# Attention and MLP on one core: a f32 first k half, a split first q half, and another order for the first batch

## The chip, the core and the metric

The kernel runs on one core of a Trainium2 chip. The metric is device time in microseconds (us); lower is better. The core has five engines that run side by side, each with its own list of instructions taken in order: TensorE (PE in the profile; its weight loads are PEld), VectorE (DVE), ScalarE (ACT), GpSimd (POOL) and SyncE (SP). An engine waits for another one, or for a transfer (DMA), by a semaphore. Transfers are issued here from POOL, SP and ACT.

## The reference

Eight batches of eight heads go through local attention (512 positions, window 32 to each side) with 32 global positions per head; both the local and the global rows attend to the global keys too. The result, 4352 tokens of 512 values, goes through an MLP with the activation h·sigmoid(1.702 h):

```python
s_g = scale * q_g @ [k_g, k_l].T ;  out_g = softmax(s_g) @ [v_g, v_l]
s_l = scale * [q_l @ k_g.T , where(|i-j| <= 32, q_l @ k_l.T, -1e9)]
out_l = softmax(s_l) @ [v_g, v_l]
x = concat([out_g, out_l], seq).transpose(0, 2, 1, 3).reshape(4352, 512)
h = x @ w_in ;  out = (h * sigmoid(1.702 h)) @ w_out        # 512 -> 2048 -> 512
```

The inputs and the output are float32; the kernel multiplies in bfloat16.

## The kernel before, in words

The work is cut into 16 "quads": batch b, four heads u = 0 or 1. In the code `a` is the quad with u = 0, `c` the one with u = 1. Each quad goes through these steps, each a method of `Quad`:

- `Tk`, `Tq` (L263, L266): VectorE turns k and q in blocks, from the loaded `rk`, `rq` into `kT` and `qt`. `ext` (L275): four small copies put the global queries at both ends of `qt`.
- `S(0)`, `S(1)` (L293, L302): scores of two windows each on TensorE, into the four-bank PSUM tile `s4`, of which there is one (`psS`, one buffer). Only the first `S(1)` of all uses four single banks instead (`split=True`).
- `X` (L314, L312): exponentials on ScalarE into `e`; `M` (L321): VectorE multiplies them by `mask`.
- `K`, `XK` (L326, L332): scores of the global keys and their exponentials `ek`.
- `U(0)`, `U(1)`, `U(2)` (L341, L349): sums of the exponentials, and the two halves of e·v, each into one bank `ov`; `Gm` (L367): the global rows, into `og`.
- `R` (L373 to L377): reciprocals of the sums; `XL` (L382): the normalised x into `xL`; `G` (L387 to L390): the same for the global rows into `xG`.

The single banks (`kb`, `ov`, `og`, `hp`, `op`) come from one pool, `psP`, of four buffers taken in turn; a user of a bank waits for what read it four allocations before.

When a batch has its `xL`, the MLP follows. `h_step(i, fc)` for fc = 0 to 15 makes one 128-wide slice of h (L414, four matmuls), its tanh on ScalarE (`th`, L421) and the product on VectorE (`gT`, L422). In batch 0 the first four slices are different: `h_mm` puts them into one `s4` tile, tanh runs on two slices at once (L524) and `act4` (L458) makes two slices of `gT` in one instruction. `o_mm` (`osteps`) multiplies `gT` by w_out (L439): a step (tci, f4) is four matmuls, of fc = 4·f4 to 4·f4+3, into the bank `op` of row block tci; after the fourth step ScalarE copies the bank to `ob` (L446) and SP stores it. From batch 1 on, `phase_o` lays the attention of the next batch between the output matmuls of this one.

The order on each engine is the order of the calls in the source (`manual_schedule`). Nearly all loads are issued on POOL and cast to bf16 on the way (L84, L88, L97, L223, L225); each of them waits until the one eight places before it has landed. At the start the q half of batch 0, u = 0, comes as f32 (`q32`) on the ACT queue and ScalarE casts it (L465); `load_g32` brings the global rows of batches 0 and 1 as f32, and `cast_g32` (L121) casts them on VectorE. `make_mb` (L170) copies mask rows `mk` to four partition groups, `make_mask` (L177) spreads them into `mask`. `keep` issues matmuls without use (L152): 17 at the start, four before the first `S(1)`. The lines around the first batch that the change rewrites:

```python
    a.U(0)
    a.U(1)
    c.S(1)
    c.X(1)
    a.U(2)
    c.K()
    c.XK()
```

Of the kernel before, what the change touches and what calls it, by code (L numbers as in the profile page):

```python
# [12 lines left out]
F32 = mybir.dt.float32  # L13
BF16 = mybir.dt.bfloat16
FP8 = mybir.dt.float8e4
AF = mybir.ActivationFunctionType
# [4 lines left out]
def kernel(  # L21
# [12 lines left out]
    nc = tc.nc  # L34

    B, H, Sl, D = q_l.shape
# [20 lines left out]
    ld = ctx.enter_context(tc.tile_pool(name="ld", bufs=3))  # L57
# [7 lines left out]
    kf = k_l.rearrange("b (u j) (c r t) d -> b j r u c (t d)", j=4, c=4, t=4)  # L65
# [5 lines left out]
    loaded = {}  # L71

    def load(b, us=(0, 1), kq=True):
        if b not in loaded:
            loaded[b] = (ld.tile([128, 2, 4, 4 * D], BF16, name="rk"),
                         ld.tile([128, 2, 16 * D], BF16, name="rq"))
        if kq:
            for j in (0, 2, 1, 3):
                for u in us:
                    load_k(b, u, j)  # L80
            load_q(b, us)

    def load_k(b, u, j):
        nc.gpsimd.dma_start(out=loaded[b][0][32 * j : 32 * j + 32, u], in_=kf[b, j][:, u])  # L84

    def load_q(b, us):
        s = slice(us[0], us[-1] + 1)
        nc.gpsimd.dma_start(out=loaded[b][1][:, s], in_=qf[b][:, s])  # L88
# [14 lines left out]
    def load_g(lo, hi):  # L103
        nc.gpsimd.dma_start(out=rkg[:, lo:hi, :], in_=kgf[:, lo:hi, :])
        nc.gpsimd.dma_start(out=rqg[:, lo:hi, :], in_=qgf[:, lo:hi, :])
        nc.gpsimd.dma_start(out=rvg[:, lo:hi, :], in_=vgf[:, lo:hi, :])

    g32 = {}

    def load_g32(b, names, hold=False, eng=None):  # L110
        for name, s in (("q", qgf), ("k", kgf), ("v", vgf)):
            if name in names:
                t = g32[b, name] = consts.tile([128, 2, D], F32, name="g32%s%d" % (name, b))
                if hold:
                    nc.vector.memset(t[:, :, 0:1], 0.0)
                (eng or nc.sync).dma_start(out=t, in_=s[:, 2 * b : 2 * b + 2, :])

    def cast_g32(b, names):
        for name, t in (("q", rqg), ("k", rkg), ("v", rvg)):
            if name in names:  # L120
                nc.vector.tensor_copy(t[:, 2 * b : 2 * b + 2, :], g32[b, name])  # L121

    load_g32(0, "qk")

    q32 = ld.tile([128, 16 * D], F32, name="q32", bufs=1)
    nc.scalar.dma_start(out=q32, in_=qf[0][:, 0])
    load_g32(0, "v", eng=nc.scalar)
    load(0, kq=False)
    for j in range(4):
        load_k(0, 0, j)  # L130


    mk = consts.tile([32, 208], BF16)
    nc.vector.memset(mk, 1.0)
    for sg, base in ((1, 2 * W + 3), (-1, -3)):
        nc.gpsimd.affine_select(
            out=mk, in_=mk, pattern=[[-sg, 208]], compare_op=ALU.is_ge,
            fill=0.0, base=base, channel_multiplier=4 * sg,
        )
    load(0, (1,))  # L140

    w_in_sb = wts.tile([128, 2, NKC, d_ff // 2], BF16)
    w_out_sb = wts.tile([128, FC, d_model], BF16)
# [20 lines left out]
    mb = consts.tile([128, 16, 12], BF16)  # L164
# [2 lines left out]

    def make_mb():
        for k in range(4):
            nc.scalar.activation(mb[32 * k : 32 * k + 32],  # L170
                                 mk[:, 3 - k : 195 - k].rearrange("p (r t) -> p t r", t=16), AF.Copy)

    def make_mask():
        at = 0
        for c, (r0, nr) in enumerate(WIN):
            lo = r0 - 8 * c + 2
            nc.scalar.activation(  # L177
                mask[:, c // 2, at : at + 16 * nr].rearrange("p (t r) -> p t r", t=16),
                mb[:, :, lo : lo + nr], AF.Copy)
            at = (at + 16 * nr) % LW  # L180
# [7 lines left out]
    for i in range(2):  # L188
        v = consts.tile([128, 2, 4, 4, D + 2], BF16, name="v%d" % i)
# [14 lines left out]
    def transpose_g(lo, hi):  # L204
        for dst, s in ((kgT, rkg), (qgT, rqg)):
            nc.vector.transpose(dst[:, lo:hi, :32], s[:, lo:hi].bitcast(F32))

    def expand_g(b, which):
        qs = slice(2 * b, 2 * b + 2)
        kgBD, vgBD = GB[b % 3]  # L210
        out_, in_ = (kgBD, kgT[:, qs].bitcast(BF16)) if which == 0 else (vgBD[:, :, :, :D], rvg[:, qs])
        nc.vector.tensor_mul(
            out_,
            in_.rearrange("p n (o w) -> p n o w", o=1).to_broadcast([128, 2, 4, D]),
            bdm.rearrange("p (o j) w -> p o j w", o=1).to_broadcast([128, 2, 4, D]),
        )

    def load_rest():
        load_v(0)
        for part in range(2):  # L220
            cs = slice(part * (d_ff // 2), (part + 1) * (d_ff // 2))
            for u in range(2):
                nc.gpsimd.dma_start(out=w_in_sb[:, part, 2 * u : 2 * u + 2, :], in_=w_in_r[u][:, :, cs])  # L223
        for g4 in range(4):
            nc.gpsimd.dma_start(  # L225
                out=w_out_sb[:, 4 * g4 : 4 * g4 + 4, :].rearrange("p (g e) m -> p g (e m)", e=2),
                in_=w_out_r[:, 2 * g4 : 2 * g4 + 2, :])
            if g4 == 1:
                load(1, (0,))
        load(1, (1,))  # L230
        load_v(1, (0,))
        load_v(1, (1,))
        load(2)
# [7 lines left out]
    class Quad:  # L241
# [20 lines left out]
            cs = slice(128 * cs[0], 128 * cs[-1] + 128)  # L262
            nc.vector.transpose(self.kT[:, cs], rk[:, cs])  # L263

        def Tq(self):
            nc.vector.transpose(self.qt[:, 4:20, :].rearrange("p t r -> p (t r)"),  # L266
                                loaded[self.b][1][:, self.u].bitcast(F32))

        def T(self):
            self.Tk()  # L270
# [136 lines left out]
    def width(i):  # L407
        return TB if i < B else B * Sg
# [3 lines left out]
    def h_mm(i, fc, hp, kcs):  # L412
        for kc in kcs:
            nc.tensor.matmul(hp[:, : width(i)], lhsT=w_in_c[:, fc // 8, kc, fc % 8 // 2, :, fc % 2],  # L414
                             rhs=(xL[i] if i < B else xG)[:, kc, :],
                             start=(kc == 0), stop=(kc == NKC - 1))
# [8 lines left out]
    def h_step(i, fc):  # L425
        if fc == 0:
            gTs[i] = moe.tile([128, FC, TB], BF16, name="gT")
        hp = pbank("hp")
        h_mm(i, fc, hp, range(NKC))
        h_act(i, fc, hp)  # L430
# [25 lines left out]
    def act4(i, hf):  # L456
        f = slice(2 * hf, 2 * hf + 2)
        nc.vector.scalar_tensor_tensor(gTs[i][:, f, :], in0=th4s[i][:, f], scalar=1.0, in1=pts[i][:, f],  # L458
                                       op0=ALU.add, op1=ALU.mult)
# [2 lines left out]

    a, c = Quad(0), Quad(1)
    rk, rq = loaded[0]
    nc.scalar.activation(rq[:, 0], q32, AF.Copy)  # L465
    make_mb()
    make_mask()
    cast_g32(0, "qk")
    transpose_g(0, 2)
    a.ext()  # L470
    a.Tq()
    a.Tk((0, 1))
    a.Tk((2, 3))
    load_g32(1, "qkv", hold=True)
    load_rest()
    a.S(0)
    a.X(0)
# [1 line left out]
    a.S(1, split=True, warm=4)  # L479
    a.X(1)  # L480
    c.ext()
    cast_g32(0, "v")
    c.Tk()
    expand_g(0, 1)
    a.K()
    a.XK()
    a.M(0)
    c.Tq()
    c.S(0)
    c.X(0)  # L490
    a.M(1)
    a.U(0)
    a.U(1)
    c.S(1)
    c.X(1)
    a.U(2)
    c.K()
    c.XK()
    a.Gm()
    a.R()  # L500
    c.M(0)
    a.XL(0)
    a.XL(1)
    c.M(1)
    a.G()
    gTs[0] = moe.tile([128, FC, TB], BF16, name="gT")
    pt = pts[0] = psS.tile([128, 4, 512], F32, name="s4")
    for fc in (0, 1):
        h_mm(0, fc, pt[:, fc, :], (0, 1))
    for unit in range(3):  # L510
        c.U(unit)
    for fc in (2, 3):
        h_mm(0, fc, pt[:, fc, :], (0, 1))
    c.R()
    c.XL(0)
    c.XL(1)
    c.Gm()
    for kc in (2, 3):
        for fc in range(4):
            h_mm(0, fc, pt[:, fc, :], (kc,))  # L520
    th4 = th4s[0] = ld.tile([128, 4, TB], F32, name="th4", bufs=1)
    for hf in range(2):
        f = slice(2 * hf, 2 * hf + 2)
        nc.scalar.activation(th4[:, f], pt[:, f], AF.Tanh, scale=0.851)  # L524
    act4(0, 0)
    c.G()

    for fc in range(4, FC):
        h_step(0, fc)
        if fc == 8:  # L530
            cast_g32(1, "qkv")
        if fc == 11:
            transpose_g(2, 4)
    load_g(4, 8)
    load_v(2)
    load(3)

    def osteps(i, *sts):
        for tci, f4 in sts:
            o_mm(i, 4 * tci + f4)  # L540

    nq = {1: (Quad(2), Quad(3)), 2: (Quad(4), Quad(5))}
    a, c = nq[1]
    a.T()
    a.ext()
    act4(0, 1)
    expand_g(1, 0)
    c.ext()
    expand_g(1, 1)
    osteps(0, (0, 1), (1, 1), (2, 1), (0, 0))  # L550
    a.S(0)
    a.X(0)
    a.M(0)
    osteps(0, (1, 0), (2, 0))
    a.S(1)
    a.K()
    a.X(1)
    a.XK()
    a.M(1)
    osteps(0, (0, 2), (1, 2), (2, 2), (0, 3))  # L560
    c.T()
    c.S(0)
    c.X(0)
    c.M(0)
    osteps(0, (1, 3), (2, 3))
    c.S(1)
    c.K()
    c.X(1)
    c.XK()
    c.M(1)  # L570
    for unit in range(3):
        a.U(unit)
    a.Gm()
    a.R()
    a.XL(0)
    a.XL(1)
    a.G()
    c.UG()
    c.RXG()
    osteps(0, (3, 0), (3, 1), (3, 2), (3, 3))  # L580
    a, c = nq[2]
# [116 lines left out]
```

## Time and profile before

| What | us |
|---|---|
| median of 7 runs (lowest, highest) | 324.58 (322.83, 325.47) |
| the profiled execution, its own time | 322.73 |
| its span, first to last instruction | 321.0 |
| TensorE busy | 302.3 (94%) |
| VectorE busy | 214.4 (67%) |
| ScalarE busy | 167.2 (52%) |
| first attention score on TensorE starts | 7.63 |
| first `hp` slice (fc = 4 of batch 0) starts | 26.10 |
| first output matmul starts | 37.73 |
| first `hp` slice of batch 1 starts | 63.24 |

The span is what the profile covers; about 1.7 us of the execution's own time lie around it. A line of the profile names the engine, the line of the kernel, the operation, what it writes and reads, its shape, and in brackets how long the engine stood idle before it and what ended that. Times of instructions are from the start of the span. A matmul of 512 columns is shown as 379 ns long, but they overlap: sixteen of them run in 3.47 us (46.23 to 49.70), 0.217 us each.

### The profile page before, as it was taken

To read this page: it belongs to the slowest core of one execution; us is meant where nothing else is said; L and a number is where in the kernel's file an instruction comes from. 1 tells how busy PE (TensorE), PEld (TensorE's weight loads), DVE (VectorE), ACT (ScalarE), POOL (GpSimd) and SP (SyncE) were. 2 spreads that over 40 slices of the span, in tenths; PEclk is the share of its full clock that TensorE was granted. 3 is DMA by queue.
4 is the path that set the end of the run, shared out by engine and by line. 5 is a ranking of instruction groups with operands and counts; after the bars stand their busy time and mean duration, and the time that the engine had idled before them with its cause. 6 is when DMAs were issued, how large, how long until landed. Compare 5 with 4: busy or idle time off the path is not lost.

```text
span 321.0 us, 7295 instructions
## 1 busy us (share of the span) xinstructions
PE 302.3 (94%) x2956; PEld 147.7 (46%) x2997; DVE 214.4 (67%) x465; ACT 167.2 (52%) x252; POOL 79.0 (25%) x129
## 2 busy tenths in 40 slices
PE   8498988899999999999999999999999999999994
PEld 3253434444554454544554455445454454445551
DVE  7865954979766877678865876687857855484320
ACT  5725546077345655476446744565537733563421
POOL 8822596477019000720037000300000000000000
PEclk9979999999999999999999999999999999999999
DMA  8999999999929402990149311900211011101122
GB/s 156 165 201 207 205 119 147 176 147 128 124 65 156 76 10 60 104 156 4 42 69 166 59 35 45 120 2 6 61 36 34 2 35 50 51 0 31 36 65 65
DMA packets 59840, 27.40 MB, mean 85 GB/s; under 512 B 43168, under 2 KB 51360, under 8 KB 59808
## 3 DMA queue, kind: packets, MB, share of 16 engines
q0 software_dynamic: 51504, 17.11, 48.9%
q1 hardware_dynamic: 7888, 9.25, 10.7%
q10 hardware_dynamic: 416, 0.59, 0.6%
q8 instruction: 23, 0.38, 0.5%
q14 instruction: 9, 0.07, 0.1%
HBM read 35.13 MB, written 8.91 MB: 137 GB/s over the span
## 4 chain that ended last, share of the span: by engine, by line
PE 80%; DMA 7%; POOL 4%; DVE 3%; ACT 2%; issue 1%; POOLq 0%; DVEq 0%
PE op L439 35%; PE hp L414 32%; DMA w_out_sb<-in_moe_w_out_dram 5%; PE s L293 5%; PE ov L349 3%; PE ov L341 3%; POOL rk L84 2%; PE kb L326 2%; DMA rk<-in_k_l_dram 2%; ACT e L314 1%; POOL v L97 1%; POOL w_in_sb L223 1%; ACT ob L446 1%; DVE xL L382 1%; DVE sT L373 1%
## 5 line engine op out<-in xcount | busy, mean ns | idle before, releaser
L439 PE MATMUL op<-w_out_sb,gT 128*128 128x512 bf16 x516 | 122.2, 379 | 3.4 <-DVE gT L458 1.1
L422 DVE SCALAR_TENSOR_TENSOR gT<-th,hp 128x512 bf16<-128x512 f32 (+1 forms) x140 | 91.2, 656 | 47.1 <-ACT th L421 46.4
L414 PE MATMUL hp<-xL,w_in_sb 128*128 128x512 bf16 x487 | 108.2, 379 | 1.6 <-DVE xg L389 1.1
L421 ACT ACTIVATE th<-hp 128x512 f32<-128x512 f32 (+1 forms) x140 | 79.9, 573 | 43.2 <-PE hp L414 39.1
L414 PEld LDWEIGHTS <-w_in_sb 128*128 128x128 bf16 x576 | 56.0, 98 | 65.9 <-DVE xg L389 1.6
L439 PEld LDWEIGHTS <-gT 128*128 128x128 bf16 x544 | 51.9, 98 | 62.9 <-issue 4.0
L314 ACT ACTIVATE e<-s 128x1712 bf16<-128x1712 f32 x31 | 49.5, 1596 | 31.6 <-PE s L293 25.1
L446 ACT ACTIVATE ob<-op 128x512 f32<-128x512 f32 x34 | 20.2, 597 | 65.4 <-PE op L439 56.7
L97 POOL DMA_DIRECT2D v<-in_v_l_dram x36 | 27.0, 759 | 98.6 <-PE og L367 94.6
L84 POOL DMA_DIRECT2D rk<-in_k_l_dram x64 | 34.8, 550 | 19.1 <-DMA v<-in_v_l_dram 6.1
L321 DVE TENSOR_TENSOR e<-e,mask 128x1408 bf16<-128x1408 bf16 x32 | 28.0, 874 | 15.5 <-ACT e L314 15.3
L373 DVE STREAM_TRANSPOSE sT<-ov 128x512 f32<-128x512 f32 x16 | 11.4, 714 | 20.8 <-PE ov L349 20.8
L382 DVE TENSOR_TENSOR xL<-ov,rs 128x512 bf16<-128x512 f32 x32 | 20.7, 686 | 3.9 <-PE ov L349 2.3
L293 PE MATMUL s<-q,kT 32*128 32x200 bf16 (+1 forms) x512 | 21.4, 286 | 0.7 <-DVE q L266 0.7
L349 PE MATMUL ov<-e,v 128*32 128x192 bf16 (+1 forms) x512 | 15.7, 243 | 2.7 <-DMA v<-in_v_l_dram 2.7
L293 PEld LDWEIGHTS <-kT 32*128 32x128 bf16 x512 | 10.8, 96 | 10.7 <-issue 6.9
L349 PEld LDWEIGHTS <-v 128*32 128x32 bf16 x512 | 11.8, 98 | 6.6 <-issue 3.3
L341 PE MATMUL ov<-ek,vgBD 128*32 128x512 bf16 x128 | 12.7, 386 | 1.1 <-DVE xL L382 1.1
L377 DVE STREAM_TRANSPOSE rs<-rT 128x512 f32<-128x512 f32 x16 | 11.4, 712 | 0.6
L263 DVE STREAM_TRANSPOSE kT<-rk 128x512 f32<-128x512 f32 (+1 forms) x17 | 11.3, 668 | 0.0
L266 DVE STREAM_TRANSPOSE q<-rq 128x512 f32<-128x512 f32 x16 | 10.8, 673 | 0.0
L326 PE MATMUL kb<-q,kgBD 128*128 128x512 bf16 x29 | 9.4, 396 | 1.0 <-ACT e L312 0.7
(61 smaller groups left out, 148.7 us busy)
## 6 DMA issues: line engine op xcount, KB each, us to landing
out_dram<-ob SPq DMA_DIRECT2D x136, 64.0 KB, 1.8
rk<-in_k_l_dram POOLq DMA_DIRECT2D x64, 64.0 KB, 4.0
v<-in_v_l_dram POOLq DMA_DIRECT2D x28, 128.0 KB, 4.7
rq<-in_q_l_dram POOLq DMA_DIRECT2D x6, 512.0 KB, 7.2
w_in_sb<-in_moe_w_in_dram POOLq DMA_DIRECT2D x4, 512.0 KB, 11.2
w_out_sb<-in_moe_w_out_dram POOLq DMA_DIRECT2D x4, 512.0 KB, 12.8
rq<-in_q_l_dram POOLq DMA_DIRECT2D x3, 256.0 KB, 7.8
q<-in_q_l_dram ACTq DMA_DIRECT2D x1, 512.0 KB, 3.6
```

What stands on the lines that cost most here:

```text
L84: nc.gpsimd.dma_start(out=loaded[b][0][32 * j : 32 * j + 32, u], in_=kf[b, j][:, u])
L97: nc.gpsimd.dma_start(out=vtiles[b % 2][p, s, :, :, :D], in_=vf[b, t][:, hs])
L293: nc.tensor.matmul(ps[j][:, off : off + n * nr], lhsT=self.k[p, 128 * c : 128 * c + 128, e], rhs=self.q[p, t0 : t0 + n, r0 : r0 + nr, e], ...
L314: nc.scalar.activation(e[:, :, :RW], self.ps[:, :, :RW], AF.Exp, scale=scale)
L321: nc.vector.tensor_mul(e, e, mask[:, rnd : rnd + 1, :].to_broadcast([128, 4, LW]))
L349: nc.tensor.matmul(ov[32 * j : 32 * j + 32, :].rearrange("p (t r) -> p t r", t=16)[:, :, r0 : r0 + nr], lhsT=lv, rhs=self.E[c // 2][:, j, ...
L382: nc.vector.tensor_mul(self.x[:, 2 * self.u + h, :], self.st[1 + h], self.st["rs"])
L414: nc.tensor.matmul(hp[:, : width(i)], lhsT=w_in_c[:, fc // 8, kc, fc % 8 // 2, :, fc % 2], rhs=(xL[i] if i < B else xG)[:, kc, :], start=( ...
L421: nc.scalar.activation(th[:, :n], hp[:, :n], AF.Tanh, scale=0.851)
L422: nc.vector.scalar_tensor_tensor(gTs[i][:, fc, :n], in0=th[:, :n], scalar=1.0, in1=hp[:, :n], op0=ALU.add, op1=ALU.mult)
L439: nc.tensor.matmul(op, lhsT=gTs[i][:, fc, tci * 128 : tci * 128 + 128], rhs=w_out_sb[:, fc, :], start=(first and fc == 4 * f4), stop=(fc = ...
L446: nc.scalar.activation(ob, op, AF.Copy, scale=0.5)
```

## The change

It rewrites the prologue and the order of the calls of the first batch and a half; the loop from batch 1 on (`phase_o` and after) is untouched.

- **Loads.** The k half of batch 0, u = 0, is no longer cast on the way by four POOL loads but loaded as f32 (`k32`) by four loads on SP, the first that SP issues. Half of it is cast by ScalarE, half by VectorE. The global q and k of batch 0 move from SP to ACT, behind `q32`; the global v moves from ACT to SP. The POOL queue begins with the four k loads of u = 1. The global loads of batch 1 are called later, and `cast_g32` of batch 1 goes to ScalarE.
- **First q half.** Cast and turned in two pieces of 512 columns.
- **Mask rows.** The four copies of `make_mb` go from ScalarE to VectorE.
- **Order of the first batch.** `c.S(1)` goes ahead of `a.U(1)`, `c.K` ahead of it; `a.R` earlier; `c.M(1)` ahead of `a.XL`; the first `h_mm` all after `c.U`; `a.G` and `c.G` ahead of the first `act4`; the second tanh pair and `act4(0, 1)` from after the `h_step` loop to its place behind fc = 12.
- **First output phase.** The steps (tci, f4) are taken so that row blocks 0, 1 and 2 end one after the other. `c.T` goes ahead of `a.M(1)`, `c.M(1)` behind `a.R`.

```diff
     def cast_g32(b, names):
...
-                nc.vector.tensor_copy(t[:, 2 * b : 2 * b + 2, :], g32[b, name])
-
-    load_g32(0, "qk")
-
+                if b:
+                    nc.scalar.activation(t[:, 2 * b : 2 * b + 2, :], g32[b, name], AF.Copy)
+                else:
+                    nc.vector.tensor_copy(t[:, 2 * b : 2 * b + 2, :], g32[b, name])
+
+    load(0, kq=False)
     q32 = ld.tile([128, 16 * D], F32, name="q32", bufs=1)
+    k32 = ld.tile([128, 4, 4 * D], F32, name="k32", bufs=1)
     nc.scalar.dma_start(out=q32, in_=qf[0][:, 0])
-    load_g32(0, "v", eng=nc.scalar)
-    load(0, kq=False)
     for j in range(4):
-        load_k(0, 0, j)
+        nc.sync.dma_start(out=k32[32 * j : 32 * j + 32], in_=kf[0, j][:, 0])
+    load_g32(0, "qk", eng=nc.scalar)
+    load_g32(0, "v")
+    for j in range(4):
+        load_k(0, 1, j)
...
-    load(0, (1,))
+    load_q(0, (1,))
...
     def make_mb():
         for k in range(4):
-            nc.scalar.activation(mb[32 * k : 32 * k + 32],
...
+            nc.vector.tensor_copy(mb[32 * k : 32 * k + 32],
...
-    nc.scalar.activation(rq[:, 0], q32, AF.Copy)
+    def cast_q(hf):
+        f = slice(512 * hf, 512 * hf + 512)
+        nc.scalar.activation(rq[:, 0, f], q32[:, f], AF.Copy)
+
     make_mb()
+    cast_q(0)
+    cast_q(1)
+    nc.scalar.activation(rk[:, 0, 2:4], k32[:, 2:4], AF.Copy)
     make_mask()
     cast_g32(0, "qk")
     transpose_g(0, 2)
     a.ext()
-    a.Tq()
+    nc.vector.tensor_copy(rk[:, 0, 0:2], k32[:, 0:2])
+    a.Tq(0, 8)
     a.Tk((0, 1))
+    a.Tq(8, 16)
     a.Tk((2, 3))
-    load_g32(1, "qkv", hold=True)
     load_rest()
...
-    cast_g32(0, "v")
-    c.Tk()
-    expand_g(0, 1)
+    c.T()
     a.K()
     a.XK()
     a.M(0)
-    c.Tq()
     c.S(0)
     c.X(0)
+    cast_g32(0, "v")
+    expand_g(0, 1)
     a.M(1)
+    load_g32(1, "qkv", hold=True)
     a.U(0)
-    a.U(1)
+    c.K()
+    c.XK()
+    a.R()
     c.S(1)
     c.X(1)
+    a.U(1)
     a.U(2)
-    c.K()
-    c.XK()
     a.Gm()
-    a.R()
     c.M(0)
+    c.M(1)
     a.XL(0)
     a.XL(1)
-    c.M(1)
-    a.G()
...
-    for fc in (0, 1):
-        h_mm(0, fc, pt[:, fc, :], (0, 1))
     for unit in range(3):
         c.U(unit)
-    for fc in (2, 3):
+    c.R()
+    for fc in range(4):
         h_mm(0, fc, pt[:, fc, :], (0, 1))
-    c.R()
     c.XL(0)
     c.XL(1)
-    c.Gm()
     for kc in (2, 3):
         for fc in range(4):
             h_mm(0, fc, pt[:, fc, :], (kc,))
+    a.G()
+    c.Gm()
...
+    tanh2(0)
+    c.G()
     act4(0, 0)
-    c.G()
-
     for fc in range(4, FC):
         h_step(0, fc)
-        if fc == 8:
+        if fc == 7:
             cast_g32(1, "qkv")
-        if fc == 11:
+        if fc == 10:
             transpose_g(2, 4)
+        if fc == 12:
+            tanh2(1)
+            act4(0, 1)
...
-    act4(0, 1)
+    osteps(0, (0, 1), (0, 0), (1, 1), (1, 0))
     expand_g(1, 0)
     c.ext()
     expand_g(1, 1)
-    osteps(0, (0, 1), (1, 1), (2, 1), (0, 0))
     a.S(0)
     a.X(0)
     a.M(0)
-    osteps(0, (1, 0), (2, 0))
+    osteps(0, (0, 2), (0, 3))
     a.S(1)
     a.K()
     a.X(1)
     a.XK()
+    c.T()
     a.M(1)
-    osteps(0, (0, 2), (1, 2), (2, 2), (0, 3))
-    c.T()
+    osteps(0, (1, 2), (1, 3))
     c.S(0)
     c.X(0)
     c.M(0)
-    osteps(0, (1, 3), (2, 3))
+    osteps(0, (2, 0), (2, 1))
     c.S(1)
     c.K()
     c.X(1)
     c.XK()
-    c.M(1)
     for unit in range(3):
         a.U(unit)
     a.Gm()
     a.R()
+    c.M(1)
     a.XL(0)
     a.XL(1)
     a.G()
+    osteps(0, (2, 2), (2, 3))
     c.UG()
     c.RXG()
```

Left out of the diff: `Tq` takes a range of columns, and `tanh2(hf)` holds the tanh instruction of L524 that a loop over hf held before.

More of the change, by code (lines that the diff above doesn't have):

```diff
@@ L169, in make_mb @@
         for k in range(4):
-            nc.scalar.activation(mb[32 * k : 32 * k + 32],
-                                 mk[:, 3 - k : 195 - k].rearrange("p (r t) -> p t r", t=16), AF.Copy)
+            nc.vector.tensor_copy(mb[32 * k : 32 * k + 32],
+                                  mk[:, 3 - k : 195 - k].rearrange("p (r t) -> p t r", t=16))
     def make_mask():
@@ L263, in Tk, with Tq @@
             nc.vector.transpose(self.kT[:, cs], rk[:, cs])
-        def Tq(self):
-            nc.vector.transpose(self.qt[:, 4:20, :].rearrange("p t r -> p (t r)"),
-                                loaded[self.b][1][:, self.u].bitcast(F32))
+        def Tq(self, lo=0, hi=16):
+            nc.vector.transpose(self.qt[:, 4 + lo : 4 + hi, :].rearrange("p t r -> p (t r)"),
+                                loaded[self.b][1][:, self.u].bitcast(F32)[:, 32 * lo : 32 * hi])
         def T(self):
@@ L520, with tanh2 @@
             h_mm(0, fc, pt[:, fc, :], (kc,))
+    a.G()
+    c.Gm()
     th4 = th4s[0] = ld.tile([128, 4, TB], F32, name="th4", bufs=1)
-    for hf in range(2):
+    def tanh2(hf):
         f = slice(2 * hf, 2 * hf + 2)
         nc.scalar.activation(th4[:, f], pt[:, f], AF.Tanh, scale=0.851)
+    tanh2(0)
+    c.G()
     act4(0, 0)
-    c.G()
     for fc in range(4, FC):
         h_step(0, fc)
-        if fc == 8:
+        if fc == 7:
             cast_g32(1, "qkv")
-        if fc == 11:
+        if fc == 10:
             transpose_g(2, 4)
+        if fc == 12:
+            tanh2(1)
+            act4(0, 1)
     load_g(4, 8)
```

## The prediction

> **What bounds the kernel now.** First the page: how busy each engine is and in which fortieths (8.0 us each) of the span.
>
> ```profile
> PE 302.3 (94%) x2956; PEld 147.7 (46%) x2997; DVE 214.4 (67%) x465; ACT 167.2 (52%) x252; POOL 79.0 (25%) x129
> ...
> PE   8498988899999999999999999999999999999994
> ```
>
> TensorE is full from slice 8 on. The table of stages, cut where a marker of the first batch starts, and TensorE's waits ahead of 64 us and behind it:
>
> ```profile
> 0.00:7.63 7.63, 6.16 (x17) 2.15 (x18) 5.60 (x36) 4.42 (x6) 6.33 (x16) 1.00 0.82 157
> 7.63:16.13 8.50, 4.39 (x80) 2.20 (x81) 7.02 (x19) 6.33 (x11) 7.46 (x11) 1.00 1.66 164
> 16.13:26.10 9.97, 9.11 (x170) 4.79 (x173) 5.75 (x11) 2.28 (x3) 2.19 (x4) 0.83 1.12 205
> 26.10:37.73 11.63, 10.48 (x49) 4.60 (x48) 8.83 (x20) 8.29 (x13) 5.42 (x9) 1.00 1.16 206
> 37.73:63.24 25.51, 21.78 (x295) 10.73 (x296) 17.19 (x38) 9.70 (x12) 17.98 (x29) 1.00 1.40 155
> 63.24:321.02 257.78, 250.40 (x2351) 123.19 (x2383) 170.00 (x344) 136.22 (x207) 39.66 (x62) 1.00 0.44 64
> ```
>
> ```profile
> PE ov L349 <- DMA v<-in_v_l_dram: 2.7, 1, 2.7
> PE ov L341 <- DVE xL L382: 1.1, 1, 1.1
> PE hp L414 <- DVE xg L389: 1.1, 1, 1.1
> PE op L439 <- DVE gT L458: 1.1, 1, 1.1
> PE s L293 <- DVE q L266: 0.7, 1, 0.7
> PE kb L326 <- ACT e L312: 0.7, 1, 0.7
> PE ov L341 <- DVE sT L373: 0.6, 1, 0.6
> ```
>
> ```profile
> PE op L439 <- DVE xL L382: 0.4, 1, 0.4
> PE op L439 <- issue: 0.2, 1, 0.2
> ```
>
> Columns of the table: length, then busy time of PE, PEld, DVE, ACT, POOL, granted clock, DMA share (16 engines), GB/s. After 63.24 TensorE waits 0.6 us in 258: only what happens before can change the time. There the waits add up to 10.1 us behind the warm-up's start, and the clock column shows 0.83 in one stage (0.57 between 16 and 20 us). The timeline says where each comes from:
>
> ```profile
> 4.45 1.06 ACT L465 ACTIVATE rq<-q 128x1024 bf16<-128x1024 f32 x1 [1.43 <-DMA q<-in_q_l_dram]
> 5.32 0.34 DVE L121 CAST rkg<-g32k 128x128 bf16<-128x128 f32 x1 [0.37 <-DMA g32k<-in_k_g_dram]
> 7.63 0.66 PE L293 MATMUL s<-q,kT 32*128 32x200 bf16 x16
> ...
> 16.13 0.49 PE L349 MATMUL ov<-e,v 128*32 128x160 bf16 x16 [2.71 <-DMA v<-in_v_l_dram]
> 17.66 1.60 ACT L314 ACTIVATE e<-s 128x1712 bf16<-128x1712 f32 x1 [3.56 <-PE s L302]
> ```
>
> S(0) starts 2.3 us after the cast of the global k, which its landing released. At 16.13 `a.U(1)` waits for v, and `c.S(1)`, needing no v, stands behind it in TensorE's order, so ScalarE sits idle 3.56 us. The chain of waits leads back over the loads instead, to `kT` at 39.16; but the k loads for it, issued from 15.05, took 16.8 us at most, and VectorE's own preceding `gT` (38.56, 0.69) ends there. So VectorE's order sets 39.16, not the queue.
>
> **What the Trainium skill says.** *TensorE: Matmul & The Clock Gate*, "Part 1: The HAM clock gate": an idle window of about 3.4 us halves the clock. Agrees: 2.71 idle, then 0.57. *DMA: Bandwidth & Descriptors*, "Issuing engines are not separate DMA queues": another issuing engine saves issue time alone. The trace fits: a k load takes POOL 0.55 us to issue (0.46 on SP), and the DMA share is over 1 from 8 to 60 us. *VectorE: DVE Perf Modes*, "Mode 2×_2P": an f32 copy in SBUF can run two elements a cycle, at 0.96 GHz 0.27 us for 512, else 0.53. The trace speaks for the slow rate: the casts of 128 start at 33.49, 33.62 and 33.76, 0.135 apart. I take 0.53.
>
> **Part by part.** *Start.* VectorE's work from the cast of the global k to S(0) was 2.34 us. Added: the 512-column k cast, 0.53 (as above; 0.27 to 0.6 as bounds; ScalarE's takes 1.06/2). Splitting the q turn adds nothing: two of 256 columns start 0.33 apart, one of 512 takes 0.63 to the next. The global k now comes third on ACT behind 512 KB of q, while 512 KB of k share the engines: before, q took 3.6 us to land and the global k 4.0, at 5.3. Bounds for its new landing are 5.3 (no sharing) and 6.9 (all that is ahead, 0.6 MB more at the 380 GB/s that the first 14 us reach at best); I take 5.9. S(0) then starts at 5.9 + 2.34 + 0.53 = 8.8, **1.15 later**. The mask rows cost ScalarE 2.21; on VectorE some 4 x 0.2 by the element rate, under the wait for g32q (from 4.55; without it +0.8). ScalarE's q casts, k cast (0.53) and mask (1.07) end near 7.9, ahead of X(0), which before waited 0.3 for the mask: X(0) 9.5 instead of 8.62.
>
> *v and POOL.* Four issues of 0.55 leave POOL's list ahead of q and v, so v comes about 2.2 earlier, 13.8; at worst 16.0 as now. The batch-1 globals (three SP loads, before at 7.89 to 9.29) go behind v; SP has nothing else then, and their casts come at 28. Weights follow v earlier by the same 2.2 or less; all that I use below is due after its present landing, so the gain needs none of it. Output stores queue behind them on SP, from 40 us only.
>
> *First batch.* ScalarE from X(0) at 9.5 has the rows X(0) 1.48, X(1) 1.66, XK 0.7, c.X(0) 1.6, c.XK 0.65; c.S(1) fits at 15.1, so c.X(1) starts at 15.9 instead of 17.66. c.M(1) ends 1.6 + 0.9 + 0.2 later, 18.6. Queued behind it on VectorE now: a.XL(0), a.XL(1), 0.65 each, to 19.9, and `c.U(1)`, `c.U(2)` wait for their banks: last U done 20.4. c.R 1.73 and c.XL 1.3 end at 22.95. `h_mm`: eight matmuls hidden under c.R, then eight x 0.217 behind the two XL: 24.1; c.Gm 0.35: the first `hp` starts at **24.45 instead of 26.10** (−1.65). The clock stays full, no idle stretch being over 1.2.
>
> *h slices.* 12 x 0.865 = 10.4 to 34.85: **−2.88**, as the 1.09 wait for `og` is gone (c.G comes first). ScalarE: 12 x 0.6 + 0.97 twice + casts 3 x 0.3 = 10.0, just under. VectorE: 12 x 0.69 + 1.22 twice + 0.44 + 0.7 = 11.9, over; it ends 37.1. With four banks TensorE doesn't feel it until 34.
>
> *Output phase.* Sixteen output matmuls (3.47) to 38.3; `Tk`, `Tq`, `ext` after VectorE's 37.1 end at 38.9: S(0) there, 0.6 wait. The step (0,3) at 40.4 needs w_out's last quarter, which even unmoved (issued 29.25, 9.8 to land) is there at 39.1. a.S(1) waits for X(0) of 1.6, 41.35; c.S(0) for a.X(1), XK and one `ob` copy, 44.3; c.S(1) for c.X(0), 46.75; the U's and steps (2,2), (2,3) run to 51.6; c.U and c.Gm to 53.5; row block 3 to 57.4. The 21.78 of work gets 22.55, since block 0 now frees its bank first and three `op` banks are no longer held at once. Batch 1 starts at 57.4 instead of 63.24: **−5.84**.
>
> Such a count leaves too little idle. The stage before had 3.7; I give 1.8 instead of 0.8, so −4.8. Span 316.2, profiled execution 317.9 (it was 322.73); the median lies 1.85 above that execution: **319.8**.
>
> **Rivals.** *A: VectorE becomes the bound.* The inserted `act4` (1.22) delays `gT`, so that banks come late and TensorE waits for them among the h slices, too. For: 11.9 of VectorE work against 10.4. Against: `act4` is moved from ahead of the first scores (40.73), where it cost the 1.1 wait of `op`, and nothing is added. TensorE then ends the slices with VectorE at 36.9 instead of 34.85: gain 2.8, 321.8. *B: late start.* If the global k lands at 7.9, S(0) is at 10.8, and since ScalarE runs from X(0) to c.X(1) without a gap, nothing makes it up: gain 2.8, 321.8. For: q, k and the globals share the engines at their busiest; against: only 0.5 MB is new there. *C: hidden anyway.* The earlier v may be worth nothing: with c.S(1) and its wait for ScalarE ahead of it, `a.U(1)` comes at 16.0 even with v at 13.8. That leaves 319.8 as it is, and says that the order of calls, not the loads, brings it. *D, slower: the clock gate.* From 8 to 25 us TensorE works in short bursts, and each window of 3.4 us at half clock costs up to 1.7. Two there, beside the one now, take back 3.4: 323.2, no change. Four cost 6.8 against 4.8: 326.6. It gets slower from the third on. For: one window was lost before. Against: the stage from 7.63 with 52% busy kept 1.00 in spite of gaps of 0.7, and only the 2.71 gap was followed by half clock.
>
> **How the numbers follow.** Forecast, C included, 0.60 (own range 317.5 to 321.3); A 0.12; B 0.10; D with two windows 0.10, with more 0.08. Low end: the count without the added idle, 318.7, less 0.6 for a global k at 5.3 and 0.3 for a cast at 0.27, and less 0.9 because medians of such runs differ by some 0.3% (the seven spread over 2.6): 316.9. High end: 319.8, plus 1.0 for a global k at 6.9, plus 1.9 if the output stage stays as idle as before: 322.7. That takes in A and B and leaves D out. About 0.5%, 1.6 us, is what a measurement can tell from no change: faster 0.82, same 0.10, slower 0.08.
>
> **What would show it.** Right: S(0) near 8.8, no v wait, c.X(1) before 16.5, `hp` at 24.5, output at 35, batch 1 at 57 to 59, clock 1.00, and 258 us from there on. Wrong: S(0) beyond 10, waits of `hp` for `gT`, a clock of 0.5, or a stage after batch 1 longer than 257.8.

## The result and the profile after

The median is **319.84 us** (318.44 to 321.02, 12 runs) against 324.43 us (322.35 to 326.17, 31 runs) for the kernel before: a ratio of 0.9865, 95% interval 0.9843 to 0.9887. The forecast of the median was 319.8. The total was hit, but not by way of every step: the first batch starts later and runs at a lower clock than forecast, and the step from one profiled execution to the median was too large by nearly as much.

First the busy times and the fortieths of the profile after.

```profile
PE 304.4 (95%) x2956; PEld 148.5 (47%) x2997; DVE 215.6 (68%) x468; ACT 166.7 (52%) x253; POOL 76.9 (24%) x125
...
PE   8589999999999999999999999999999999999993
```

The number of matmuls is the same, yet TensorE is busy 2.1 us longer: matmuls at half clock last longer. The table of stages says where, cut at the same markers as before (first score, first `hp` slice, first output matmul, batch 1's first `hp`); the columns are length, busy time of PE, PEld, DVE, ACT, POOL, granted clock, DMA share, GB/s.

```profile
0.00:11.21 11.21, 6.65 (x18) 2.41 (x19) 7.35 (x42) 4.02 (x8) 9.70 (x19) 0.97 1.15 181
11.21:28.67 17.46, 15.69 (x250) 7.48 (x252) 12.56 (x30) 7.95 (x11) 4.94 (x9) 0.72 1.26 198
28.67:39.04 10.37, 10.32 (x56) 4.72 (x49) 8.86 (x16) 8.50 (x16) 4.71 (x8) 1.00 1.20 203
39.04:61.23 22.19, 21.34 (x293) 10.72 (x296) 17.07 (x40) 10.04 (x13) 17.68 (x29) 1.00 1.51 157
61.23:319.30 258.07, 250.40 (x2351) 123.18 (x2383) 169.75 (x344) 136.21 (x207) 39.89 (x62) 1.00 0.45 64
```

Against before (7.63, 18.47, 11.63, 25.51, 257.78) that is +3.58 at the start, −1.01 from the first score to `hp`, −1.26 in the h slices, −3.32 in the output phase, +0.26 behind it (the last row runs 0.03 past the last instruction): −1.75 in all, which is the difference of the two spans. The medians differ by 4.6. The two profiles are no typical pair: that of before took 322.73 us (median 324.43), that of after 321.02, the highest of its twelve runs. TensorE's waits ahead of 62 us:

```profile
PE s L298 <- DVE q L271: 3.1, 1, 3.1
PE w L157 <- DVE warm L153: 1.5, 1, 1.5
PE ov L354 <- DVE e L326: 0.7, 1, 0.7
PE kb L331 <- ACT e L317: 0.4, 1, 0.4
```

The wait for v (2.7), the two for `xL` and `xg` (1.1 each) and the one for `gT` (1.1) are gone. What was 0.7 ahead of the first score is 3.1. The timeline around it:

```profile
6.51 0.29 DVE L124 CAST rqg<-g32q 128x128 bf16<-128x128 f32 x1 [0.47 <-DMA g32q<-in_q_g_dram]
8.63 0.23 DVE L124 CAST rkg<-g32k 128x128 bf16<-128x128 f32 x1 [1.83 <-DMA g32k<-in_k_g_dram]
...
9.68 0.48 DVE L482 CAST rk<-k 128x512 bf16<-128x512 f32 x1
...
11.21 0.90 PE L298 MATMUL s<-q,kT 32*128 32x200 bf16 x16 [3.10 <-DVE q L271]
...
20.65 0.57 PE L354 MATMUL ov<-e,v 128*32 128x160 bf16 x16
```

VectorE stands still 1.83 us until the global k lands, at 8.60, where before it landed at 5.29. The turn of q and k is queued behind that cast, and the first score waits for the turn. The last piece of the f32 k lands at the same time, at 8.59; its cast comes a little later in VectorE's order, at 9.68. `a.U(1)` at 20.65 waits for nothing; v had landed at 14.33.

### The profile page after: what moved, and what is told of

It is laid out like the page before. It is cut to its first block, busy times and chain, and to the rows that moved or that the text cites. A ratio compares the mean times of both kernels' runs of the same rounds, so it can differ in the third digit from the quotient of the medians.

```text
span 319.3 us, 7303 instructions
## 1 busy us (share of the span) xinstructions
PE 304.4 (95%) x2956; PEld 148.5 (47%) x2997; DVE 215.6 (68%) x468; ACT 166.7 (52%) x253; POOL 76.9 (24%) x125
## 4 chain that ended last, share of the span: by engine, by line
PE 84%; DMA 7%; POOL 3%; DVE 2%; issue 2%; ACT 1%; POOLq 0%; DVEq 0%; ACTq 0%
PE op L444 35%; PE hp L419 34%; PE s L298 5%; DMA w_in_sb<-in_moe_w_in_dram 4%; PE ov L354 4%; PE ov L346 3%; DMA rq<-in_q_l_dram 3%; PE kb L331 2%; POOL v L97 1%; POOL rk L84 1%; PE og L372 1%; PE s L307 1%; ACT th L426 1%; DVE sT L378 0%; POOL w_in_sb L228 0%
## 5 line engine op out<-in xcount | busy, mean ns | idle before, releaser
L84 POOL DMA_DIRECT2D rk<-in_k_l_dram x60 | 32.6, 555 | 16.5 <-DMA v<-in_v_l_dram 4.3
L298 PE MATMUL s<-q,kT 32*128 32x200 bf16 (+1 forms) x512 | 22.2, 294 | 3.6 <-DVE q L271 3.1
L271 DVE STREAM_TRANSPOSE q<-rq 128x512 f32<-128x512 f32 (+1 forms) x17 | 10.9, 638 | 0.0
```

Source lines behind the costliest of these rows:

```text
L298: nc.tensor.matmul(ps[j][:, off : off + n * nr], lhsT=self.k[p, 128 * c : 128 * c + 128, e], rhs=self.q[p, t0 : t0 + n, r0 : r0 + nr, e], ...
```

## The experiments

Theory 1 held that the order of the calls brings the gain, and that the new loads only make the start late, because the global k waits behind q and k. Its rivals held that the new loads bring part of it (v early), and that the clock gate decides. Unless a section says otherwise, a kernel is the kernel after with one part changed. Each ratio is to runs of the kernel before beside it, whose medians lay between 324.06 and 324.43. All in one table, the markers from each kernel's profile; "S" is the first score, the stages are S to `hp`, and the first output matmul to batch 1's `hp`:

| kernel | median us (lowest to highest, runs) | ratio to before, 95% | S at | S to `hp` | output stage |
|---|---|---|---|---|---|
| before | 324.43 (322.35 to 326.17, 31) | | 7.63 | 18.47 | 25.51 |
| after | 319.84 (318.44 to 321.02, 12) | 0.9865 (0.9843 to 0.9887) | 11.21 | 17.46 | 22.19 |
| old_loads | 317.59 (317.12 to 319.98, 6) | 0.9803 (0.977 to 0.9835) | 8.32 | 16.17 | 22.77 |
| loads_alone | 324.13 (322.92 to 325.31, 22) | 1.0007 (0.9991 to 1.0023) | 10.77 | 16.23 | 25.51 |
| old_attn | 319.42 (318.42 to 321.12, 6) | 0.9883 (0.9839 to 0.9926) | 10.67 | 15.86 | 22.17 |
| old_loads_attn | 319.35 (318.61 to 320.81, 6) | 0.9874 (0.9838 to 0.991) | 8.33 | 18.76 | 22.22 |
| old_output | 322.07 (320.8 to 324.15, 22) | 0.9944 (0.9924 to 0.9963) | 10.65 | 17.51 | 24.43 |
| old_act4 | 323.65 (321.02 to 324.93, 14) | 0.9978 (0.9947 to 1.001) | 10.67 | 17.46 | 26.49 |
| globals_first | 321.2 (320.1 to 322.47, 6) | 0.9901 (0.987 to 0.9932) | 12.70 | 16.56 | 23.11 |
| warm_more | 319.44 (318.97 to 320.05, 5) | 0.9855 (0.9824 to 0.9885) | 10.66 | 15.27 | 22.90 |
| best | 317.28 (316.98 to 317.6, 4) | 0.9806 (0.9765 to 0.9847) | 7.74 | 17.82 | 22.17 |

### The same kernel again

No edit: a second profile of after.

> The changed kernel once more, for a second profile. Theory 1 (the first scores wait for the global k, which lands behind q and k; how late depends on how the queues share the engines in that run): the landing of the global k and the start of S(0) differ from the first profile (8.6 and 11.21) by up to 2 us, and with the half clock windows the time lies between 318.4 and 321.0. Theory 2 (the start is the same each time, the spread comes from the clock alone): S(0) within 0.3 us of 11.21.

It took 319.45 us: S at 10.80, S to `hp` 16.37, output stage 22.18, 258.03 behind it. The late start is no chance of one profile. The stage S to `hp` is: 16.37 here with a clock of 0.79, 17.46 in the first with 0.72.

And before, a second profile:

> The kernel before once more, for a second profile. Theory 1 (most of its spread is half clock in the first 60 us, in windows of 3.4 us): S(0) again within 0.3 of 7.63 and v within 0.5 of 16.0, the stage after batch 1 has started again 257.8, and the time is 321.8 to 322.5 with no half clock there, 1.0 to 1.5 more for each window. Theory 2 (the loads differ from run to run): v or S(0) differs by 1 us or more.

It took 325.20 us: S at 7.74, S to `hp` 19.75, output stage 26.59, 257.78 behind it. Both long stages ran at a lower clock (0.74 for 11 us ahead of `hp`, 0.94 in the output stage). So the first profile of before was one with little lost clock, and 18.47 and 25.51 are low for it.

### The loads of before in the new order

```diff
-    load(0, kq=False)
+    load_g32(0, "qk")
...
     nc.scalar.dma_start(out=q32, in_=qf[0][:, 0])
+    load_g32(0, "v", eng=nc.scalar)
+    load(0, kq=False)
     for j in range(4):
-        nc.sync.dma_start(out=k32[32 * j : 32 * j + 32], in_=kf[0, j][:, 0])
-    load_g32(0, "qk", eng=nc.scalar)
-    load_g32(0, "v")
-    for j in range(4):
-        load_k(0, 1, j)
+        load_k(0, 0, j)
...
-    load_q(0, (1,))
+    load(0, (1,))
...
-    nc.scalar.activation(rk[:, 0, 2:4], k32[:, 2:4], AF.Copy)
-    nc.vector.tensor_copy(rk[:, 0, 0:2], k32[:, 0:2])
```

> Changed kernel with the k half of batch 0, u = 0, cast again by four POOL loads and the globals first on SP, so without the f32 k half and its casts. Theory 1 (order of calls brings the gain, the new loads cost): global k lands at 5.3, S(0) at 7.7, c.X(1) near 17 instead of 20.35, time 317.0 to 318.0, a ratio to before of 0.978. Theory 2 (relief of the POOL queue and the earlier v bring the gain): v lands at 16 again, time 322 to 324.

317.59 us, 2.25 below after. The stage rows of this kernel:

```profile
0.00:8.32 8.32, 5.56 (x18) 2.13 (x19) 6.73 (x41) 3.39 (x7) 7.01 (x17) 1.00 0.83 153
8.32:24.49 16.17, 12.96 (x251) 6.87 (x252) 12.48 (x30) 7.80 (x11) 8.53 (x13) 1.00 1.38 175
```

The start is 2.9 us earlier and the clock is full. v lands at 15.1, hardly sooner than the 16.0 of before, and TensorE doesn't wait for it. The reason for the late start of after is seen in the DMA issues of the first 9 us (KB each, and us from issue to landing), before and then after:

```profile
q<-in_q_l_dram ACTq DMA_DIRECT2D x1, 512.0 KB, 3.6
rk<-in_k_l_dram POOLq DMA_DIRECT2D x8, 64.0 KB, 2.8
...
g32k<-in_k_g_dram SPq DMA_DIRECT2D x2, 64.0 KB, 4.1
```

```profile
q<-in_q_l_dram ACTq DMA_DIRECT2D x1, 512.0 KB, 4.6
k<-in_k_l_dram SPq DMA_DIRECT2D x4, 128.0 KB, 5.3
rk<-in_k_l_dram POOLq DMA_DIRECT2D x4, 64.0 KB, 6.2
...
g32k<-in_k_g_dram ACTq DMA_DIRECT2D x1, 64.0 KB, 6.9
```

The global k is 64 KB; behind 512 KB of q on its queue and beside 512 KB of k on SP it takes 6.9 us instead of 4.0 (the 4.1 is a median that takes in the load for batch 1). The loads near it are slower too: q took 4.6 for 3.6, and POOL's first four k loads, issued at the same times in both, took 5.6 to 6.4 us for 3.2 to 4.3 (the 2.8 above is over eight). That fits what the Trainium skill states in *DMA: Bandwidth & Descriptors*, "Issuing engines are not separate DMA queues": transfers from whatever engine run on the same 16 DMA engines and interleave.

### The new loads in the order of before

This is the kernel before with the new loads and casts of k, and nothing else of the change:

```diff
-    load_g32(0, "qk")
-
+    load(0, kq=False)
     q32 = ld.tile([128, 16 * D], F32, name="q32", bufs=1)
+    k32 = ld.tile([128, 4, 4 * D], F32, name="k32", bufs=1)
     nc.scalar.dma_start(out=q32, in_=qf[0][:, 0])
-    load_g32(0, "v", eng=nc.scalar)
-    load(0, kq=False)
     for j in range(4):
-        load_k(0, 0, j)
+        nc.sync.dma_start(out=k32[32 * j : 32 * j + 32], in_=kf[0, j][:, 0])
+    load_g32(0, "qk", eng=nc.scalar)
+    load_g32(0, "v")
+    for j in range(4):
+        load_k(0, 1, j)
...
-    load(0, (1,))
+    load_q(0, (1,))
...
+    nc.scalar.activation(rk[:, 0, 2:4], k32[:, 2:4], AF.Copy)
...
+    nc.vector.tensor_copy(rk[:, 0, 0:2], k32[:, 0:2])
```

> The kernel before with the new loads of the start alone (f32 k half on SP with its two casts, globals q and k on ACT, v on SP); order of calls, q cast in one piece and mask rows on ScalarE as before. Theory 1 (they delay the start, and the earlier v pays back only the part that v was waited for): S(0) at 10.7, no wait for v, c.X(1) at 18.8 to 19.4 instead of 17.66, time 1.0 to 1.8 us above before, ratio 1.003 to 1.006. Theory 2 (the relief of the POOL queue is worth more than the start): ratio 0.995 or less.

1.0007 (0.9991 to 1.0023), beside 27 runs of before with a median of 324.06: no difference, where a loss was expected. The profile shows two effects against each other. S is 3.1 later (10.77), and S to `hp` is 2.2 shorter (16.23 for 18.47), since v is there when `a.U(1)` comes; `hp` starts at 27.00, between the 26.10 and 27.49 of the two profiles of before. The largest wait of TensorE in it, and its first step that needs v:

```profile
PE s L295 <- DVE kT L265: 2.7, 1, 2.7
```

```profile
17.39 0.49 PE L351 MATMUL ov<-e,v 128*32 128x160 bf16 x16
```

The 2.7 us have only changed place, from v to the first score. v landed at 14.35 here, but TensorE doesn't ask for it before 17.39, and by then it would be there with the loads of before too (16.00 and 16.48 in the two profiles of before). So the late start alone would hide the wait, and this run doesn't show that the earlier v is worth anything.

### The attention order of before, with the new and with the old loads

Calls from `a.S(0)` to the `h_mm`s as before; the output phase and the moved `act4` stay as in after.

```diff
+    load_g32(1, "qkv", hold=True)
     load_rest()
...
     a.U(0)
-    c.K()
-    c.XK()
-    a.R()
+    a.U(1)
     c.S(1)
     c.X(1)
-    a.U(1)
     a.U(2)
+    c.K()
+    c.XK()
...
-    for fc in range(4):
+    for fc in (2, 3):
```

> Changed kernel with the first batch's attention in the order of before, up to and with the order of c.G and act4 (the batch-1 globals are called early again with it). Theory 1 (the order takes c.S(1) out from behind the wait for v): since S(0) now starts after 10 and v lands at 14.3, the v wait is gone in this kernel anyway, and what is lost is the wait for og and some order: 320.5 to 321.3. Theory 2 (the order is worth what was forecast whatever the start): 321.5 to 322.8.

319.42 us, where 0.7 to 1.5 more than after was expected. With the new loads the new attention order brings nothing (after is 0.4 slower, its range inside the other's). There is no v wait that it could take away: v lands at 13.76, and TensorE asks for it at 16.92.

> The kernel with the old loads and, besides, the first batch's attention in the order of before. Theory 1 (that order matters where S(0) is early and v late, as the prediction had it): a.U(1) waits for v to about 15.3, c.X(1) starts at 16.5 instead of 15.27, time 318.2 to 319.0, ratio 0.983. Theory 2 (worth nothing, as with the new loads): 317.6, ratio 0.980.

This one has the loads of before as well: 319.35 us, 1.8 more than old_loads. The wait is back in its list, v having landed at 16.87:

```profile
PE ov L352 <- DMA v<-in_v_l_dram: 2.7, 1, 2.7
```

The four kernels together: with the loads of before, the new attention order brings 1.8; with the new loads it brings nothing. The order lets TensorE do other work while v is on its way. With the new loads TensorE has stood still ahead of the first score, and comes to v when it has landed. Whether the earlier landing of v is worth anything by itself stays open, since no run has it together with an early start. With the order in place the loads only cost.

### The output order of before

```diff
-    osteps(0, (0, 1), (0, 0), (1, 1), (1, 0))
     expand_g(1, 0)
     c.ext()
     expand_g(1, 1)
+    osteps(0, (0, 1), (1, 1), (2, 1), (0, 0))
...
-    osteps(0, (0, 2), (0, 3))
+    osteps(0, (1, 0), (2, 0))
...
```

> Changed kernel with the first output phase in the order of before (steps, c.T and c.M(1) where they were); act4 and all ahead of it stay. Theory 1 (this order brings the largest part): the stage from the first output matmul to batch 1 takes 24.4 instead of 22.2 us, with waits for sT and xL back; time 321.6 to 322.4. Theory 2 (what the stage gained came from act4 being out of it): 319.8 to 320.4.

322.07 us, 2.2 above after. The output stage is 24.43, again at full clock, and TensorE waits in it for `xL` 1.1 more than in after, for `sT` 0.3 more and for `op` 0.4: banks that come free late, as forecast.

### The second `act4` back in its place

```diff
     tanh2(0)
+    tanh2(1)
...
-        if fc == 12:
-            tanh2(1)
-            act4(0, 1)
...
+    act4(0, 1)
     osteps(0, (0, 1), (0, 0), (1, 1), (1, 0))
```

> Changed kernel with the second tanh pair ahead of the h slices and act4(0, 1) behind a.T and ext, ahead of the output steps, as before. Theory 1: the wait of the output matmuls for gT is back, 1.1 us or more, since (0,0) comes second now: 320.8 to 321.6. Theory 2 (moved work only, VectorE is as late either way): 319.8.

323.65 us, 3.8 above after, where some 1 to 2 were expected. The wait that comes back, and its output stage with a cut of 3.4 us inside it:

```profile
PE op L444 <- DVE gT L463: 2.8, 1, 2.8
```

```profile
38.71:65.20 26.49, 23.39 (x298) 10.86 (x296) 17.30 (x39) 9.94 (x12) 21.80 (x35) 0.94 1.39 151
43.90:47.30 3.40, 3.40 (x23) 1.09 (x21) 0.06 (x1) 0.00 (x0) 3.40 (x7) 0.50 1.12 127
```

The wait for `gT` is 2.8 and not the 1.1 of before, since in the new order the step (0,0), which needs the late slices, comes second instead of fourth; and then 3.4 us run at half clock, though TensorE is busy throughout. That these 3.4 us come from the 2.8 of idle time is likely by the order of events, but not shown, and the one doesn't always bring the other: three of its fourteen runs, with the same order of calls and so presumably the same wait, had a mean clock of 0.999 or more. They took 321.02 to 321.77, against 318.44 and 318.57 in the two such runs of after, so 2.5 to 3.3 of the 3.8 are there without lost clock. The two edits of the output phase seem to lean on each other: with `act4(0, 1)` late, closing row block 0 early brings little. No run has both as before and all else as after; the nearest is loads_alone, at 324.13.

### The globals first, on SP

```diff
+    load_g32(0, "qk")
...
     nc.scalar.dma_start(out=q32, in_=qf[0][:, 0])
     for j in range(4):
         nc.sync.dma_start(out=k32[32 * j : 32 * j + 32], in_=kf[0, j][:, 0])
-    load_g32(0, "qk", eng=nc.scalar)
-    load_g32(0, "v")
...
+    load_g32(0, "v", eng=nc.scalar)
```

> Changed kernel with the global q and k of batch 0 as the first two loads on SP, ahead of the f32 k half; the global v goes last on ACT. Theory 1: global k lands by 5.5, k by 8, S(0) at 9.3 or earlier (k is late instead), time 317.5 to 318.8. Theory 2 (all transfers of the start share the engines, so the last of them lands at 8.6 whatever the order): S(0) stays at 11, time 319.8.

321.2 us, 1.4 slower than after, where a gain was expected. The globals are early, and then k is late:

```profile
6.32 0.49 DVE L124 CAST rkg<-g32k 128x128 bf16<-128x128 f32 x1
...
11.21 0.43 DVE L482 CAST rk<-k 128x512 bf16<-128x512 f32 x1 [3.50 <-DMA k<-in_k_l_dram]
```

The last piece of the f32 k now lands at 11.09. So it isn't the queue of the global k alone that makes the start late. The first k half is four f32 loads of 128 KB now, where it was four casting loads that the profile counts at 64 KB each, and beside 512 KB of q they end beyond 8 us in both orders: at 8.59 in after, at 11.09 here. The first score needs the globals and k, and whichever is ready last sets it. In after, the cast of k starts 1.53 us ahead of the first score; with k at 8.59 the score could not have come before some 10.1 (an estimate from these two figures) however early the global k.

### More matmuls without use at the start

The call of `keep` at the start gets 25 instead of 17 matmuls, which fills most of the gap ahead of the first score (1.5 us of it is left).

> Changed kernel with 25 instead of 17 warm-up matmuls without use, which last to 9.5 to 11 instead of 8.1. Theory 1 (the 3.1 us gap ahead of S(0) lets the clock go to half): no half clock before 20 us, time 318.0 to 318.8, 0.004 below the changed kernel. Theory 2 (the half clock does not matter since the stage waits for ScalarE and VectorE): 319.8, or later by what the warm-up delays S(0).

```profile
10.66:25.93 15.27, 12.68 (x251) 6.72 (x252) 12.58 (x30) 7.72 (x11) 5.41 (x9) 1.00 1.30 198
```

No half clock is left, and S to `hp` is 15.27, 2.2 less than in the first profile of after and 1.1 less than in the second. So the gap does cost the clock: all five runs of this kernel have a mean clock of 0.998 or more, where after's lie between 0.981 and 1.000. The median is only 0.4 lower (319.44), which the intervals don't resolve, and the five runs (318.97 to 320.05) lie above the two of after that lost no clock (318.44 and 318.57), so something else is given back. In the profile it is the output stage, 0.7 longer (22.90), all of it at one place: from the start of the last group of `og` to the next output matmul TensorE takes 0.99 us for 0.27 in the second profile of after, and nothing that the profile shows ends this pause. The cause stays open.

### The old loads, the mask rows split over two engines

Old_loads, with the mask rows for k = 0 and 1 back on ScalarE:

```diff
+            if k < 2:
+                nc.scalar.activation(o, i, AF.Copy)
+            else:
+                nc.vector.tensor_copy(o, i)
```

> The kernel with the old loads (no f32 k half) and the mask rows split, two copies on ScalarE ahead of the q casts and two on VectorE. Theory 1 (four copies on VectorE take 1.33 us and hold up the cast of the global k by 0.8): the cast starts at 5.3, S(0) at 7.6 instead of 8.32, time 316.6 to 317.2. Theory 2 (ScalarE's mask then holds up X(0), or w_out binds the output steps): 317.6.

317.28 us (316.98 to 317.6), the lowest median of all, but only 0.3 below old_loads and not told from it. Its S is at 7.74, 0.6 earlier, as the copies on VectorE (two of them, 0.66 us; four took 1.33 in old_loads) no longer hold up the cast of the global k. But S to `hp` is 17.82, 1.65 more. Two things lengthen it: the q half of the second quad lands at 11.0 (10.6 in old_loads), and VectorE waits for it 1.69 us instead of 0.70; and the profile runs at half clock between 14.3 and 17.7. Both kernels with the loads of before and the new order (old_loads, best) lie under the kernel after.

## Why the prediction was right, and where not

The medians make one chain: before 324.4; with the new output phase, the early `act4` and the small casts, 319.35 (old_loads_attn), −5.1; with the attention order, 317.59 (old_loads), −1.8; with the new loads, 319.84, +2.25.

**Start: wrong in size.** "S(0) then starts at 5.9 + 2.34 + 0.53 = 8.8". It started at 10.65 to 11.21 in the seven profiles of kernels with these loads as they are. The term that failed is the landing of the global k, taken as 5.9 with 6.9 as the upper bound; it landed at 7.95 to 8.60 in them. The bound counted the bytes ahead of it, at the best rate of the profile of before; but the rate was not kept up: in after it is 278 to 378 GB/s for less than 2 us, from 2.7 to 4.5, and 171 to 236 from there to 9. A second term is missing from the sum: the landing of the f32 k itself, 8.25 to 8.70 in the seven profiles, which alone puts the first score at some 10 us (with the 1.53 from the start of its cast, as above). The cast (0.53 forecast) took 0.48, with 0.39 to the next. The forecast took the slower of two rates for it, from the starts of the casts of 128; the durations speak for the faster one: 0.23 us for 128 columns and 0.42 to 0.48 for 512 in after and loads_alone, so 0.5 to 0.65 ns a column, where the two rates weighed are 0.52 and 1.04. VectorE's chain from the cast of the global k to the first score took 2.58, not 2.87. Rival B, the late start, is what happened, and it took nothing from the total only because other terms erred the other way. The mask rows, forecast as 4 x 0.2, took 1.46 and still cost after nothing, as VectorE waits for `g32q` until 6.51 anyway; with the old loads the cover is thinner, and there they hold up the start.

**v and POOL: right.** Forecast 13.8, "so the gain needs none of it" (rival C); 14.33, 15.12 and 13.76 in three profiles, and never waited for. Old_loads shows that the early v isn't needed in the new order: there v lands at 15.10 and is asked for at 15.39.

**First batch: right in the work, wrong on the clock.** From S to `hp` the count gave 24.45 − 8.8 = 15.65; at full clock it is 15.27 (warm_more). "The clock stays full, no idle stretch being over 1.2" failed with the start: the gap ahead of the first score is 3.1, and the stage runs at 0.72, 17.46. In four cuts of this kernel:

```profile
10.00:14.00 4.00, 2.79 (x24) 1.13 (x28) 3.59 (x13) 1.87 (x3) 3.06 (x5) 0.57 2.08 173
14.00:18.00 4.00, 3.20 (x53) 1.60 (x48) 2.16 (x7) 3.04 (x6) 1.29 (x3) 0.50 1.13 213
18.00:21.00 3.00, 3.00 (x52) 1.19 (x44) 2.46 (x4) 2.10 (x3) 0.54 (x1) 0.53 1.09 173
21.00:24.00 3.00, 2.07 (x91) 1.44 (x81) 2.02 (x4) 1.04 (x2) 0.55 (x1) 1.00 1.13 208
```

That is rival D's mechanism in a place where it was not looked for: half clock for some 10 us, at a price of 2.2 (17.46 against 15.27). But the price doesn't go by the length: the second profile of after loses 1.1 in 6.8 us, and old_output, which has the same code up to `hp`, loses 1.05 in its only window of 3.4 us (its first `kb` starts 3.88 us after S, in warm_more 2.83). That window falls on the four matmuls without use between S(0) and S(1), behind which S(1) stands; here in warm_more and in old_output:

```profile
11.25 1.04 PE L157 MATMUL s<-warm 128*128 128x512 bf16 x4
```

```profile
11.24 1.85 PE L157 MATMUL s<-warm 128*128 128x512 bf16 x4
```

The rest of the 2.2 by which old_output's stage (17.51) exceeds warm_more's is mostly a pause of TensorE of 1.02 us within `c.U(2)` that nothing in the profile ends; old_loads has one of 0.73 at the same matmul, best one of 0.86. So not all of the spread of this stage is clock, and what these pauses are stays open.

**h slices: right.** 10.4 forecast, 10.37 measured. VectorE ended its `gT` 2.4 us after TensorE went on to the output matmuls (2.25 by the count), and no `hp` waited for it: rival A's mechanism did not come.

**Output phase: right, without the margin.** The count gave 22.55, measured 22.19 (22.18 in the second profile), of which 0.85 is idle. "Such a count leaves too little idle ... I give 1.8 instead of 0.8": the 1.0 was not needed. The parts were mis-weighed: undoing the early `act4` costs 3.8, not the 1.1 of the wait that it removed, since in the new order that wait is 2.8 and, in part, since clock is lost besides.

**The rest: 258.04 for 257.78.** It is 258.02 to 258.04 in every profile with the new loads and 257.78 to 257.79 in every one without. TensorE takes 253.13 us of it in both; the 0.25 lies behind its last matmul, after the last store is issued. Why is open.

**From the execution to the median: wrong.** "The median lies 1.85 above that execution" was a property of the profile of before, which ran 3.4 us at half clock where its second profile ran 10.2; it is not one of the kernel. For after it is −1.18. The sum against the first profile of after: start +2.4, S to `hp` +1.8, h slices 0.0, output −1.4, rest +0.3, so +3.1 on the span of 316.2; the shift to the median −3.0. Against the second profile the same terms are +2.0, +0.7, 0.0, −1.4, +0.2: +1.5, and the shift −1.5. So 319.8 is met to 0.04 through errors that cancel, one of the start and the clock, the other of the reference execution: that it is so close is luck.

## What to carry to other kernels

When a wait is gone, look whether it was removed or has only moved: with the new loads TensorE stands still ahead of the first score instead of ahead of v, and with the new order and the old loads it doesn't wait for v and waits 1.3 us ahead of the first score, at 317.6. A small transfer that much work is queued behind pays for the large ones of the same moment (6.9 us for 64 KB, where it was 4.0), so its landing time can't be taken from a profile in which they weren't there; and each transfer that the first step needs wants a landing time of its own in the sum. Before forecasting a median from one profile, see how much clock that profile had lost.

## What the runs showed of the hardware

Half clock comes in pieces of 3.41 us or multiples of it (3.4, 6.8, 10.2 in these profiles), and the Trainium skill's *TensorE: Matmul & The Clock Gate*, "Part 1: The HAM clock gate", gives the same window, about 3.4 us, as the idle time that halves the clock and as the busy time that restores it. The runs agree with the size and differ on the conditions. Half clock followed on gaps of 2.7 (loads_alone, 0.90 in the stage after it) and 3.1, as it did on the 2.71 of before that the prediction counted as agreement; and when warm_more shortened the 3.1 to 1.5, it was gone. The length of the gap didn't set the length of the slow stretch: 3.9 ahead of the first score in old_output was followed by 3.4 us, 3.1 in after by 10.2. And in best 3.4 us at half clock came with no single gap over 1.2, after short bursts with TensorE busy 2.22 of 4.30 us; old_loads, nearly the same kernel, kept full clock in its profile. What decides between the two was not settled.

The run-to-run spread goes with the clock: over 46 runs of before the mean granted clock goes from 0.977 to 0.998 and the time falls by 1.7 us for each 0.01. For after it is 1.1 for each 0.01, over 12 runs. By these two lines, which are estimates, before is at 322.0 at full clock and after at 318.85, so about 3.2 of the 4.6 us are there at full clock. The rest is lost clock: after loses a little less of it (a mean of 0.990 against 0.987), and what it loses costs it less.
